# Weight tiles 5 to 7 of the gated unit split beside the spatial products instead of the u products, in the first batch

## Chip, cores and metric

The kernel runs on one core of a Trainium2 chip, as one program launched once. The metric is the device time in microseconds (us) of one execution. Five engines work side by side and each follows its own list of instructions in order: PE (matrix products and their weight loads, PEld), DVE (vector), ACT (scalar, with the table functions), POOL, and SP, which here issues all data transfers (DMA).

## The reference, cut to what matters

Three layers follow each other on 4 batches of 576 positions. The change is in the second; the first runs interleaved with it.

```python
# 1 attention, per batch and head (8 heads of 64), with a causal mask and a decay bias
scores = scale * q @ k.T + min(-(cum_i - cum_j), 0)        # masked above the diagonal
attn = softmax(scores) @ v                                 # -> x, 576 x 512 per batch
# 2 the gated unit
h = gelu(x @ w_in)                                         # w_in 512 x 1024
u, v = h[:, :512], h[:, 512:]
v_n = layernorm(v) * g_ln
v_s = w_sg @ v_n + b_sg                                    # w_sg 576 x 576: the spatial product
x = x + (u * v_s) @ w_out                                  # w_out 512 x 512
# 3 channel mix: k = relu(xk @ w_k), v = (k * k) @ w_v, r = sigmoid(xr @ w_r), out = r * v
```

## The kernel before, in words

Every float32 operand of a product is written as a sum of two parts in a format (fp32r) that PE takes at full pace: a cast gives the high part, a subtraction (`split_lo`, L68 and L69) the low part. A product is then made of three: high by high, high by low, low by high.

The attention of two heads is one pair (`attn_pair`, L205 to L344), 16 pairs in all. The steps of a pair that the prediction names are: the transfer of kq (L217), two splits of it on POOL (L69: qa and KB), two score products per block on PE (L252, L253), the masked minimum on DVE that reads the scores and releases their bank (L277), the exponential on ACT (L285), transposes on PE (L303) with copies back (L305, L307, L313), a reciprocal of the row sums on DVE (L320), its store (L321) and three loads that spread it over the partitions (rb, L324 to L326).

The gated unit is `moe1(b)` (L372 to L480), per batch: v products with layer norm (vn is the normalised v, split in two); four u products, each in two halves of 288 columns (L438 by way of L368), with GELU made of four operations, on ACT and DVE (L499 to L502); then four spatial steps m. Step m makes two product groups sg (L454), evicts each by DVE into a tile ga (L455), multiplies ga by u on POOL (L459), casts it on ACT to gh (L460) and takes the low part gl on POOL (L462). The last loop makes the four output tiles, y, from all gh and gl and the weight tiles 4 to 7 (counted from 0).

The weights of u and of the output stand in eight tiles of 128 columns, index 0 to 3 from w_in and 4 to 7 from w_out. In batch 0 they come as float32 from HBM, are split by the chip and stored to a scratch tensor (`wscr`), from which later batches load them in one transfer (L510). That splitting is `first_wc` (L174 to L191) and `convert` (L74 to L88). It takes tiles 3 to 7 in two halves each. A half is: a transfer `wr` (L188), two activations on ACT that build a rescaled copy `wy` (L76 reads wr, L81 reads wr), two bit operations on DVE (L82 reads wr and wy, L84 works on wy), a cast on ACT into the high half of the tile (L87), and a subtraction on DVE for the low half (L69). After both halves the tile is stored (L190).

Three things set where this work stands. First, tiles ga, wr, wy, y and a few others have one tag, `tmp`, with three buffers: a new tile of the tag takes the buffer of one that has been used up, and its writer waits for the readers of that one. The weight tiles have a tag `wc`, also with three buffers. Second, the program is built by walking `moe1` as a generator, and after each of its steps attention steps of the next batch are added until they have a given share (`attention_until`, L535). Third, a scheduler reorders these instructions on each engine by its own model of their times; the order of the text is only its input. What comes before what on an engine is read from the built program.

In `moe1` before the change, tile m + 3 is made after u product m (L441), for m from 0 to 3, and tile 7 in the loop of output tiles (L465). In later batches the same call is a single load.

Of the kernel before, what the change touches and what calls it, by code (L numbers as in the profile page):

```python
# [37 lines left out]
def fused_kernel(ctx, tc, kqT, vL, s, w_in, g_ln, w_sgT, b_sg, w_out, mu_k, mu_r, w_k, w_v, w_r, out):  # L38
# [25 lines left out]
    def f32(ap):  # L64
        return ap.bitcast(F32)


    def split_lo(eng, lo, x, hi):  # L68
        eng.tensor_tensor(out=lo, in0=x, in1=f32(hi), op=ALU.subtract)  # L69
# [278 lines left out]
    def scale_pending(early):  # L348

        while pending:  # L350
            x_t, rbs = pending.pop()
            i = nc.vector.tensor_tensor(out=x_t, in0=x_t, in1=rbs, op=ALU.mult)
            if early is not None:
                after(i, early)
# [3 lines left out]
    def bank(name, free=True):  # L358

        tag = ('sc', 'tp', 'acc', 'sc', 'tp', 'acc', 'tp', 'acc')[banks[0] % 8] if free else "acc"  # L360
        banks[0] += 1
        return psum1.tile([P, 512], F32, tag=tag, name=name, bufs={'sc': 2, 'tp': 3, 'acc': 3}[tag])
# [9 lines left out]
    def moe1(b):  # L372

        GS = 1.0 if b == B - 1 else 2.0 * WS
        wcs = []
        for c in range(3):
            wcs.append(load_wc(b, c))
        xs = low.tile([P, 2, KD, S], F32R, tag="xs", name=f"xs_{b}")
        xs = [xs[:, i] for i in range(2)]

        xq = ep.tile([P, S + 1], F32R, tag="tmp", name=f"xq_{b}", bufs=3)
        xq = xq[:, :KD * P].rearrange("p (k a t) -> p k a t", k=KD, a=2)
        if pending and pending[0][0] is xT[(b, KD - 1)]:
            scale_pending(None)
        for k in range(KD):
            nc.scalar.copy(xs[0][:, k], xT[(b, k)])
            split_lo(nc.gpsimd, xs[1][:, k], xT[(b, k)], xs[0][:, k])
        for i in range(2):
            nc.vector.tensor_copy(xq[:, :, i], f32(xs[i][:, :, 512:]))
        yield 0  # L390
        v = ep.tile([P, NT, FH], F32, tag="v", name=f"v{b}")
        st6 = ep.tile([P, NT, 6], F32, tag="st6", name=f"st6_{b}")
        mv = ep.tile([P, NT, 2], F32, tag="mv", name=f"mv{b}")
        rstd = ep.tile([P, NT], F32, tag="rstd", name=f"rstd{b}")
        vn = [ep.tile([P, NT, FH], F32R, tag=f"vn{i}", name=f"vn{i}_{b}") for i in range(2)]
        for t in range(NT):
            m = TW[t]
            acc = bank(f"v{b}_{t}", b == B - 1)
            mms = []
            for k in range(KD):  # L400
                if t < 4:
                    xh, xl = (x[:, k, t * P:t * P + m] for x in xs)
                    mms += [(xh, wv[0][:, k]), (xh, wv[1][:, k]), (xl, wv[0][:, k])]
                else:
                    x2 = xq[:, k].rearrange("p a t -> p (a t)")
                    mms += [(x2, wv[0][:, k]), (x2, wv[1][:, k])]
            gemm3(acc, mms)
            if t < 4:
                gelu(b, v[:, t], acc)
            else:  # L410
                xt = ep.tile([P, S + 1], F32, tag="tmp", name=f"vx{b}", bufs=3)
                nc.scalar.copy(xt[:64, :FH], acc[64:128])
                nc.vector.tensor_tensor(out=xt[:64, :FH], in0=acc[:64], in1=xt[:64, :FH], op=ALU.add)
                gelu(b, v[:64, 4], xt[:64, :FH])
            nc.vector.bn_stats(out=st6[:m, t], in_=v[:m, t])
            nc.vector.bn_aggr(out=mv[:m, t], in_=st6[:m, t])
            nc.gpsimd.tensor_scalar_add(rstd[:m, t:t + 1], mv[:m, t, 1:2], LN_EPS * GS * GS)
            nc.gpsimd.tensor_tensor(out=rstd[:m, t:t + 1], in0=rstd[:m, t:t + 1], in1=mhalf[:m, 0:1], op=ALU.pow)
            nc.vector.tensor_scalar(out=v[:m, t], in0=v[:m, t], scalar1=mv[:m, t, 0:1], scalar2=rstd[:m, t:t + 1],
                                    op0=ALU.subtract, op1=ALU.mult)  # L420
            last_cast[0] = nc.scalar.copy(vn[0][:m, t], v[:m, t])
            if t < 4:
                split_lo(nc.vector if b == B - 1 else nc.gpsimd, vn[1][:, t], v[:, t], vn[0][:, t])
            else:

                split_lo(nc.vector, vn[0][64:128, 4], v[:64, 4], vn[0][:64, 4])
            yield len(mms) * 512 * V_W
        u = []
        for m in range(KD):
            u.append(ep.tile([P, S], F32, tag="u", name=f"u{b}_{m}", bufs=4))  # L430
            for hf in range(2):
                acc = bank(f"u{b}_{m}_{hf}", b == B - 1)
                c = slice(hf * HF, (hf + 1) * HF)
                mms = []
                for k in range(KD):
                    wh, wl = wcs[m][:, 0, k * P:(k + 1) * P], wcs[m][:, 1, k * P:(k + 1) * P]
                    mms += [(wh, xs[0][:, k, c]), (wh, xs[1][:, k, c]), (wl, xs[0][:, k, c])]
                gemm3(acc[:, :HF], mms)  # L438
                gelu(b, u[m][:, c], acc[:, :HF])
                yield 12 * 288 * U_W  # L440
            wcs.append(load_wc(b, m + 3))  # L441
        gh = ep.tile([P, KD, S], F32R, tag="v", name=f"gh{b}")
        gs = [[gh[:, m] for m in range(KD)], []]
        for m in range(KD):
            f = slice(m * P, (m + 1) * P)
            ga = ep.tile([P, S + 1], F32, tag="tmp", name=f"ga{b}_{m}", bufs=3)
            for hf in range(2):
                acc = bank(f"sg{b}_{m}_{hf}", b == B - 1)
                c = slice(hf * HF, (hf + 1) * HF)
                mms = []  # L450
                for k in range(4):
                    mms += [(vn[0][:, k, f], wsg[0][:, k, c]), (vn[0][:, k, f], wsg[1][:, k, c]), (vn[1][:, k, f], wsg[0][:, k, c])]
                mms += [(vn[0][:, 4, f], wsg[0][:, 4, c]), (vn[0][:, 4, f], wsg[1][:, 4, c])]
                gemm3(acc[:, :HF], mms)  # L454
                nc.vector.scalar_tensor_tensor(out=ga[:, c], in0=acc[:, :HF], scalar=g_sb[:, m:m + 1], in1=bsg[:, c],  # L455
                                               op0=ALU.mult, op1=ALU.add)
                yield 14 * 288 * S_W
            eng = nc.vector if b == B - 1 else nc.gpsimd
            eng.tensor_tensor(out=ga[:, :S], in0=ga[:, :S], in1=u[m], op=ALU.mult)  # L459
            last_gate[0] = nc.scalar.copy(gs[0][m], ga[:, :S])  # L460
            gs[1].append(ep.tile([P, S], F32R, tag="u", name=f"gl{b}_{m}", bufs=4))
            split_lo(eng, gs[1][m], ga[:, :S], gs[0][m])  # L462
        for m in range(KD):
            if m:
                wcs.append(load_wc(b, m + 6) if m + 6 < 8 else None)  # L465
            y = ep.tile([P, S + 1], F32, tag="tmp", name=f"y{b}_{m}", bufs=3)
            nc.gpsimd.memset(y[:, 0:1], 0.0)
            wc = wcs[4 + m]
            for hf in range(2):
                acc = bank(f"o{b}_{m}_{hf}", b == B - 1)  # L470
                c = slice(hf * HF, (hf + 1) * HF)
                mms = []
                for k in range(KD):
                    wh, wl = wc[:, 0, k * P:(k + 1) * P], wc[:, 1, k * P:(k + 1) * P]
                    mms += [(wh, gs[0][k][:, c]), (wh, gs[1][k][:, c]), (wl, gs[0][k][:, c])]
                gemm3(acc[:, :HF], mms)
                nc.vector.scalar_tensor_tensor(out=y[:, 1 + hf * HF:1 + (hf + 1) * HF], in0=acc[:, :HF], scalar=1.0 / (GS * WS), in1=xT[(b, m)][:, c],
                                               op0=ALU.mult, op1=ALU.add)
                yield 12 * 288 * O_W
            nc.sync.dma_start(out=ydram[m, :, b], in_=y)  # L480
# [23 lines left out]
    def load_wc(b, c):  # L504
        if b == 0:
            if c >= 3:
                first_wc(c)
            return wc0[c]
        wc = ew.tile([P, 2, KD * P], F32R, tag="wc", name=f"wc{b}_{c}", bufs=3)
        nc.sync.dma_start(out=f32(wc.rearrange("p a f -> p (a f)")), in_=f32(wscr[c]))  # L510
        return wc
# [261 lines left out]
    for p in range(TOK // PW):  # L773
# [7 lines left out]
        a, b, c = (psum2.tile([P, 2, 512], F32, tag="ps", name=f"ps{n}_{p}", bufs=4) for n in "abc")  # L781
# [80 lines left out]
```

## Time and profile before

| | |
|---|---|
| device time, median of 3 runs | 683.03 us (681.72 to 685.47) |
| the profiled execution, its device time | 679.44 us |
| its span | 677.7 us |
| PE busy | 645.2 us (95%) |
| DVE busy | 479.1 us (71%) |
| ACT busy | 416.0 us (61%) |
| POOL busy | 219.7 us (32%) |
| mean granted clock of PE, as a share of full speed | 0.988 |

The span runs from the first to the last instruction of the profiled execution, 1.7 us less than its device time. The profiled execution is 3.6 us faster than the median of the runs. Busy shares are means over the span: an engine can be the one that is waited for in one stretch and idle in another, so what this change can do is read from the first batch, some 120 to 190 us into the span.

Three views are used below. A row of the order of time (the timeline) gives an instruction's start in us from the span's start, its duration in us, engine, line, operation, the output and input tiles by the program's names without their numbers, shapes, how many like it in a row (x), and in brackets how long the engine had been idle before and what released it; starts and ends overlap a little, since an engine takes the next instruction while the last one drains. A row of the table of stretches gives, for one stretch, its length and the busy time of PE, PEld, DVE, ACT and POOL with counts, the granted clock of PE, the busy share of the DMA engines and the GB/s. A row of the waits gives who waited for whom, the us in total, how often, and the longest.

### The profile page before, as it was taken

The page shows a single profiled execution, that of the slowest core. Times are in us where ns is not written, and L with a number is a line of the kernel's source. Part 1 is how long each engine was busy: PE and PEld are TensorE (multiplying, and loading weights), DVE is VectorE, ACT ScalarE, POOL GpSimd, SP SyncE. Part 2 cuts the span into 40 slices and gives each one's busy share as a digit, 9 for nine tenths or more (in the row PEclk, how much of TensorE's full clock was granted, in tenths as well). Part 3 has the DMA queues.
Part 4 walks back from the last instruction along what each step waited for, and adds up shares of the span by engine and source line. Part 5 has one row for each costly group of instructions (what it writes and reads, how often), then busy time and mean ns, then how long its engine had stood idle before and what let it go on. Part 6 is the DMA issues. An engine that isn't in the chain of part 4 may idle for free.

```text
span 677.7 us, 11532 instructions
## 1 busy us (share of the span) xinstructions
PE 645.2 (95%) x3912; PEld 553.5 (82%) x3912; DVE 479.1 (71%) x995; ACT 416.0 (61%) x940; POOL 219.7 (32%) x233
## 2 busy tenths in 40 slices
PE   3869999799999999999999999999999999999997
PEld 2547676779878988877988899988888988999997
DVE  7876679986668645469644388787875959677863
ACT  5878777785558656368653285587755779543530
POOL 8556646368436459237363030000000000000000
PEclk9969999999999999999999999999999999999999
DMA  7764652455453532733510675567744593546643
GB/s 227 221 205 140 186 167 73 138 158 158 152 186 102 143 115 55 240 117 90 163 37 15 214 268 183 164 224 222 255 164 163 188 361 136 168 182 195 225 139 117
DMA packets 56459, 112.74 MB, mean 166 GB/s; under 512 B 7680, under 2 KB 20624, under 8 KB 56400
## 3 DMA queue, kind: packets, MB, share of 16 engines
q1 hardware_dynamic: 56400, 112.01, 52.3%
q8 instruction: 31, 0.51, 0.3%
q14 instruction: 28, 0.23, 0.1%
HBM read 74.46 MB, written 28.02 MB: 151 GB/s over the span
## 4 chain that ended last, share of the span: by engine, by line
PE 83%; DVE 6%; DMA 6%; ACT 2%; SPq 1%; issue 1%; POOL 0%; DVEq 0%; ACTq 0%; POOLq 0%
PE k L368 15%; PE sg L368 9%; PE pv L338 8%; PE r L368 7%; PE o L368 7%; PE psa L771 7%; PE u L368 6%; PE v L368 5%; PE tp L303 5%; PE psb L771 4%; PE sc L252 4%; PE sc L253 3%; PE psc L771 2%; DMA kq<-in_kqT_dram 1%; DMA wc<-wscr 1%
## 5 line engine op out<-in xcount | busy, mean ns | idle before, releaser
L368 PE MATMUL k<-x,wk 128*128 128x512 f32 (+1 forms) x480 | 101.4, 372 | 0.0
L368 PEld LDWEIGHTS k<-x,wk 128*128 128x128 f32 x480 | 83.6, 188 | 17.4
L252 PE MATMUL sc<-ka,qa 128*128 128x512 f32 (+3 forms) x180 | 64.0, 366 | 21.6 <-DVE mx L277 10.8
L285 ACT ACTIVATE st<-st,mx 128x128 f32<-128x128 f32 (+4 forms) x124 | 72.0, 582 | 19.3 <-DVE mx L277 18.8
L277 DVE CUSTOM_DVE_ANT_0 st<-sc,mask 128x512 f32<-128x512 f32 (+3 forms) x124 | 61.1, 503 | 27.7 <-PE sc L253 24.4
L368 PE MATMUL sg<-wsg,vn 128*128 128x288 f32 x448 | 65.2, 298 | 0.9 <-DVE u L502 0.9
L338 PE MATMUL pv<-pt,vf 128*64 128x320 f32 (+4 forms) x448 | 64.8, 366 | 0.2 <-ACT pt L305 0.2
L368 PEld LDWEIGHTS sg<-wsg,vn 128*128 128x128 f32 x448 | 60.8, 188 | 1.5 <-DVE u L502 1.1
L252 PEld LDWEIGHTS sc<-ka,qa 128*128 128x128 f32 x180 | 33.9, 189 | 32.1 <-DVE mx L277 15.1
L253 PE MATMUL sc<-KB,QB 128*128 128x512 f32 (+3 forms) x180 | 57.4, 335 | 1.0 <-DVE wv L69 1.0
L338 PEld LDWEIGHTS pv<-pt,vf 128*64 128x64 f32 x448 | 35.5, 137 | 23.5 <-issue 5.2
L303 PE MATMUL tp<-ident,st 128*128 128x128 f32 x300 | 49.5, 282 | 1.2 <-ACT st L285 1.0
L368 PE MATMUL r<-x,wr 128*128 128x512 f32 (+1 forms) x240 | 50.6, 372 | 0.0
L368 PEld LDWEIGHTS r<-x,wr 128*128 128x128 f32 x240 | 41.7, 188 | 8.8
L368 PE MATMUL v<-wv,xs 128*128 128x512 f32 x192 | 48.5, 397 | 0.0
L69 POOL TENSOR_TENSOR qa<-kq,QB 64x576 fp32r<-64x576 f32 x29 | 45.1, 1555 | 3.1 <-POOL st_f L283 1.0
L229 POOL CAST QB<-kq 64x576 fp32r<-64x576 f32 x28 | 21.1, 757 | 73.6 <-PE sc L253 44.3
L69 POOL TENSOR_TENSOR KB<-kq,ka 64x576 fp32r<-64x576 f32 x29 | 43.5, 1499 | 3.9 <-ACT ka L230 1.9
L303 PEld LDWEIGHTS tp<-ident,st 128*128 128x128 f32 x300 | 35.6, 142 | 10.6 <-ACT st L285 4.6
L368 PE MATMUL o<-gh,wc 128*128 128x288 f32 x192 | 40.8, 298 | 0.8 <-DMA wc<-wscr 0.8
L368 PEld LDWEIGHTS v<-wv,xs 128*128 128x128 f32 x192 | 35.1, 188 | 7.5 <-POOL QB L229 0.5
L368 PE MATMUL u<-xs,wc 128*128 128x288 f32 x288 | 40.9, 297 | 0.0
(188 smaller groups left out, 1451.8 us busy)
## 6 DMA issues: line engine op xcount, KB each, us to landing
wc<-wscr SPq DMA_DIRECT2D x24, 512.0 KB
kq<-in_kqT_dram SPq DMA_DIRECT2D x32, 288.0 KB
kr<-kdram SPq DMA_DIRECT2D x12, 768.0 KB
kdram<-k SPq DMA_DIRECT2D x16, 512.0 KB
yt<-ydram SPq DMA_DIRECT2D x24, 257.0 KB
vf<-in_vL_dram SPq DMA_DIRECT2D x16, 320.0 KB
ydram<-y SPq DMA_DIRECT2D x16, 288.5 KB
gt<-gdram SPq DMA_DIRECT2D x12, 384.0 KB
```

What stands on the lines that cost most here:

```text
L69: eng.tensor_tensor(out=lo, in0=x, in1=f32(hi), op=ALU.subtract)
L229: (nc.scalar.copy if hd < 2 else nc.gpsimd.tensor_copy)(qb[64:128], kq[64:128])
L252: nc.tensor.matmul(sc[:m, :c1 - c0], qa[:, q], ka[:, c0:c1], start=True, stop=False)
L253: nc.tensor.matmul(sc[:m, :c1 - c0], qb[:, q], kb[:, c0:c1], start=False, stop=True)
L277: mi = nc.vector.tensor_tensor_reduce(out=st[:, c0:c1], in0=sc[:, :n], in1=mk, op0=ALU.add, op1=ALU.min, scale=-SCALE, scalar=mx[:, 0:1] i ...
L285: e = nc.scalar.activation(st[:, :w], st[:, :w], AF.Exp, bias=mx[:, last:last + 1], scale=-1.0, accum_out=sm[:, i + 5 * (hh == 1):i + 5 * ...
L303: nc.tensor.transpose(tp[:, c:c + P], st[:, j * P:(j + 1) * P], ident)
L338: nc.tensor.matmul(acc[64 * a:64 * a + 64, o:n], vf[:, a, kk], pt, start=(kk == 0), stop=(kk == nk - 1))
L368: nc.tensor.matmul(acc, a, w_, start=(i == 0), stop=(i == n - 1))
L771: nc.tensor.matmul(ps[:, c, :HW], l, r, start=(start and i == 0), stop=(i == len(mms) - 1), skip_group_check=True)
```

## The change

In batch 0, the tiles of index 4, 5 and 6 (the fifth to the seventh) are made after the spatial steps 0, 1 and 2 instead of after the u products 1, 2 and 3. Tile 3 stays behind u product 0, tile 7 stays in the output loop. Batches 1 to 3 are written as before. The line numbers of `gelu`, the evictions and the gate grow by one to three.

```diff
@@ -438,7 +438,8 @@
                 gemm3(acc[:, :HF], mms)
                 gelu(b, u[m][:, c], acc[:, :HF])
                 yield 12 * 288 * U_W
-            wcs.append(load_wc(b, m + 3))
+            if b or m == 0:
+                wcs.append(load_wc(b, m + 3))
         gh = ep.tile([P, KD, S], F32R, tag="v", name=f"gh{b}")
@@ -460,6 +461,8 @@
             last_gate[0] = nc.scalar.copy(gs[0][m], ga[:, :S])
             gs[1].append(ep.tile([P, S], F32R, tag="u", name=f"gl{b}_{m}", bufs=4))
             split_lo(eng, gs[1][m], ga[:, :S], gs[0][m])
+            if b == 0 and m < 3:
+                wcs.append(load_wc(b, m + 4))
         for m in range(KD):
```

The built programs show what this moves. In their rows the name of a tile stands with its own number behind it: wy4_0 is the first half of tile 4, ga0_1 the gate tile of batch 0 and step 1, sc6 the scores of pair 6. The first place is DVE beside the second u product, before the change:

```order
L352 TENSOR_TENSOR xT5_1150<-xT5_1150,rb5_1360 128x576
L82 SCALAR_TENSOR_TENSOR wy4_0_1456<-wr4_0_1455,wy4_0_1456 128x256
L500 SCALAR_TENSOR_TENSOR u0_1_1419<-u0_1_1419,u0_1_1_1437 128x288
L69 TENSOR_TENSOR wcs3_1399<-wy3_1_1410,wcs3_1399 128x256
L84 SCALAR_TENSOR_TENSOR wy4_0_1456<-wy4_0_1456 128x256
L307 COPY pt2_6_1520<-tp6_0_3_1577 128x4x128
L277 ISA st6_2_4_1621,mx6_2_4_1622<-sc6_2_4_1_1629,mask2_123,mx6_2_4_1622 128x64
```

The same place in the changed program:

```order
L352 TENSOR_TENSOR xT5_1150<-xT5_1150,rb5_1360 128x576
L503 SCALAR_TENSOR_TENSOR u0_1_1419<-u0_1_1419,u0_1_1_1437 128x288
L69 TENSOR_TENSOR wcs3_1399<-wy3_1_1410,wcs3_1399 128x256
L69 TENSOR_TENSOR vn0_0_1026<-v0_1022,vn0_0_1026 64x512
L307 COPY pt2_6_1500<-tp6_0_3_1557 128x4x128
L503 SCALAR_TENSOR_TENSOR u0_2_1454<-u0_2_1454,u0_2_0_1455 128x288
L277 ISA st6_2_4_1581,mx6_2_4_1582<-sc6_2_4_1_1589,mask2_123,mx6_2_4_1582 128x64
```

The L82 and the L84 of tile 4 are gone from in front of the score eviction (L277), and the vn split and one more GELU operation stand there.

The second place is ACT at the casts gh, before the change:

```order
L87 CAST wcs6_1702<-wy6_1_1713 128x256
L460 CAST gh0_1722<-ga0_0_1723 128x576
L460 CAST gh0_1722<-ga0_1_1794 128x576
L460 CAST gh0_1722<-ga0_2_1831 128x576
L340 COPY xT7_1862<-pv7_0_2055 128x256
L305 COPY pt1_8_2185<-tp8_0_1_2218 128x384
```

In the changed program the second and the third of them stand here:

```order
L76 ACTIVATE wy5_0_1793<-wr5_0_1792 128x256
L81 ACTIVATE wy5_0_1793<-wr5_0_1792,mhalf_70 128x256
L461 CAST gh0_1662<-ga0_1_1754 128x576
L87 CAST wcs5_1791<-wy5_0_1793 128x256
L230 CAST ka16_2163<-kq16_2158 64x576
L76 ACTIVATE wy5_1_1802<-wr5_1_1801 128x256
L81 ACTIVATE wy5_1_1802<-wr5_1_1801,mhalf_70 128x256
L285 ACTIVATE st7_2_4_1918,sums1_93<-st7_2_4_1918,mx7_2_4_1919 128x576
L87 CAST wcs5_1791<-wy5_1_1802 128x256
L285 ACTIVATE st7_1_0_1985,sums1_93<-st7_1_0_1985,mx7_1_0_1986 128x128
L76 ACTIVATE wy6_0_1950<-wr6_0_1949 128x256
...
L461 CAST gh0_1662<-ga0_2_1811 128x576
```

The cast gh of step 1 stands behind the first half of tile 5, that of step 2 behind the second half and the first of tile 6; before, all weight casts were ahead of the gate casts.

The third place is SP, which issues the transfers, in the changed program; wr4 to wr6 are the halves, rc and rb the reciprocals of attention:

```order
L188 DMA wr4_1_1744<-in_w_out_dram 128x2x256
L217 DMA kq17_2173<-in_kqT_dram 128x576
L321 DMA rdram_65<-rc6_1688 9x128
L324 DMA rb6_1692<-rdram_65 64x576
L325 DMA rb6_1692<-rdram_65 64x512
L326 DMA rb6_1692<-rdram_65 64x64
L188 DMA wr5_0_1792<-in_w_out_dram 128x2x256
L190 DMA wscr_61<-wcs4_1734 128x1024
L239 DMA vf8_2170<-in_vL_dram 128x640
L188 DMA wr5_1_1801<-in_w_out_dram 128x2x256
```

Before, the first half of tile 5 stood ahead of the rc store of pair 6, and that of tile 6 directly behind it; now the first half of tile 5 is behind that store and its three rb loads.

## Rows read from the trace of the kernel before

**Rows 1.** The page's first part: busy time of each engine, share of the span, instructions.

```profile
PE 645.2 (95%) x3912; PEld 553.5 (82%) x3912; DVE 479.1 (71%) x995; ACT 416.0 (61%) x940; POOL 219.7 (32%) x233
```

**Rows 2.** Table of stretches of 10 us, three of them.

```profile
120.00:130.00 10.00, 7.79 (x59) 7.17 (x57) 9.38 (x18) 6.16 (x15) 6.42 (x7) 1.00 0.52 148
130.00:140.00 10.00, 8.80 (x51) 8.15 (x52) 8.65 (x29) 8.78 (x27) 3.01 (x4) 0.83 0.41 124
...
160.00:170.00 10.00, 10.00 (x77) 9.35 (x76) 5.94 (x13) 3.58 (x7) 9.90 (x9) 1.00 0.35 114
```

**Rows 3.** Order of time on PE, from the u products to the output products.

```profile
131.15 0.39 PE L252 MATMUL sc<-ka,qa 128*128 128x256 f32 x1 [3.35 <-DVE mx L277]
...
132.93 3.25 PE L368 MATMUL u<-xs,wcs 128*128 128x288 f32 x12
...
146.36 0.39 PE L252 MATMUL sc<-ka,qa 128*128 128x256 f32 x1 [0.42 <-DVE mx L277]
...
148.16 2.13 PE L368 MATMUL sg<-wsg,vn 128*128 128x288 f32 x14 [0.86 <-DVE u L502]
...
187.84 0.29 PE L368 MATMUL o<-gh,wcs 128*128 128x288 f32 x1
...
188.22 0.48 PE L252 MATMUL sc<-ka,qa 128*128 128x512 f32 x1
```

**Rows 4.** Order of time on DVE, around the waits of PE.

```profile
126.31 0.89 DVE L82 SCALAR_TENSOR_TENSOR wy<-wr,wy 128x256 uint32<-128x256 uint32 x1
...
127.48 1.27 DVE L69 TENSOR_TENSOR wcs<-wy,wcs 128x256 fp32r<-128x256 f32 x1
128.67 1.62 DVE L84 SCALAR_TENSOR_TENSOR wy<-wy 128x256 uint32<-128x256 uint32 x1
...
131.34 0.69 DVE L69 TENSOR_TENSOR vn<-v,vn 64x512 fp32r<-64x512 f32 x1
132.05 0.46 DVE L500 SCALAR_TENSOR_TENSOR u<-u,u 128x288 f32<-128x288 f32 x1
...
146.23 1.51 DVE L82 SCALAR_TENSOR_TENSOR wy<-wr,wy 128x256 uint32<-128x256 uint32 x1
```

**Rows 5.** Order of time on POOL, just before PE goes on at 131.15.

```profile
128.55 1.46 POOL L69 TENSOR_TENSOR qa<-kq,QB 64x576 fp32r<-64x576 f32 x1
```

**Rows 6.** Order of time on ACT: a spatial weight cast, a gate cast, tile 7.

```profile
90.59 0.67 ACT L200 CAST wsg<-wsr 128x576 fp32r<-128x576 f32 x1 [0.70 <-DMA wsr<-in_w_sgT_dram]
...
170.79 0.66 ACT L460 CAST gh<-ga 128x576 fp32r<-128x576 f32 x1
...
179.93 0.44 ACT L76 ACTIVATE wy<-wr 128x256 f32<-128x256 f32 x1 [0.76 <-DMA wr<-in_w_out_dram]
180.28 0.52 ACT L81 ACTIVATE wy<-wr,mhalf 128x256 uint32<-128x256 uint32 x1
```

**Rows 7.** Order of time on DVE: a reciprocal, a fast L82, the last L69.

```profile
144.89 0.94 DVE L320 RECIPROCAL rc<-rc 9x128 f32<-9x128 f32 x1
...
173.91 0.42 DVE L82 SCALAR_TENSOR_TENSOR wy<-wr,wy 128x256 uint32<-128x256 uint32 x1 [2.48 <-POOL gl L69]
...
183.67 0.41 DVE L69 TENSOR_TENSOR wcs<-wy,wcs 128x256 fp32r<-128x256 f32 x1
```

**Rows 8.** Order of time on POOL: the split of gl in step 3.

```profile
171.53 1.42 POOL L69 TENSOR_TENSOR gl<-ga,gh 128x576 fp32r<-128x576 f32 x1 [1.40 <-ACT gh L460]
```

**Rows 9.** Issues of transfers on SP's queue, in order of time.

```profile
87.92 0.33 SPq L196 DMA_DIRECT2D wsr<-in_w_sgT_dram  x1
...
145.86 0.30 SPq L321 DMA_DIRECT2D rdram<-rc  x1
...
148.47 0.58 SPq L326 DMA_DIRECT2D rb<-rdram  x1
...
175.57 0.38 SPq L188 DMA_DIRECT2D wr<-in_w_out_dram  x1
```

**Rows 10.** Waits of PE over the whole span: the last long one.

```profile
PE o L368 <- DMA wc<-wscr: 0.8, 1, 0.8
```

## Prediction

> **What bounds the kernel now.** The page's first part comes first: PE is busy 95% of the span of 677.7 us [rows 1], so the change can win or lose only PE's idle time and the clock. Next, the table of stretches of 10 us shows where idle lies in the first batch: PE is busy 7.79 and 8.80 us of the stretches 120 to 130 and 130 to 140, in the second at a granted clock of 0.83 (a part of it at 1.2 instead of 2.4 GHz); from 160 to 170 it is full and DVE is at 5.94 [rows 2]. The u products are made in the first two, most spatial products in the third. Then the order of time on PE gives the waits: 3.35 us before the score products at 131.15, 0.42 at 146.36, 0.86 at 148.16, all released by DVE; the twelve u products at 132.93 took 3.25 us, the fourteen at 148.16 only 2.13 [rows 3]. DVE's order of time says what stood in front of the release at 131.15: an L82 and an L84 of weight tile 4 (0.89 and 1.62 us) and the last L69 of tile 3 (1.27) [rows 4].
>
> **What the change does.** Tiles 4, 5 and 6 are converted in two halves each; a half is one transfer (SP), L76, L81 and L87 on ACT, and L82, L84 and L69 on DVE. Nothing is added; the order shows these behind evictions of the spatial products instead of between those of u. What each part is worth:
>
> *The wait at 131.15.* On DVE the L82 and the L84 leave (2.51 us) and the L69 of vn and an L500 come ahead of the release (0.69 and 0.46) [rows 4], so it comes about 1.3 us earlier; I take 1.2, PE goes on at 130.0. Bounds: nothing gained, if the vn split then waits for POOL, whose qa split ends at 130.01 [rows 5]; 3.35, if DVE is never late.
>
> *The waits 0.42 and 0.86.* They stand by an L82 of 1.51 us on DVE at 146.23 [rows 4], which goes. Gain 1.28; bounds 0 and 1.28.
>
> *The clock.* 0.17 of 10 us is 1.7 us [rows 2]. A wait of 3.35 came before that fall; behind the one of 0.86 the products at 148.16 ran at full pace [rows 3]. The wait that I leave, 2.15, is between them: I take half the loss as gone, bounds 0 and 1.7.
>
> *The new chain.* This decides how much of that stays. ga, wr and wy tiles share three buffers. In the changed program both halves of wr4 and all ga tiles but the first have one, the first ga and then the four halves of wr5 and wr6 the second, every wy the third. So the halves follow each other: a transfer is issued when L82 of the half before has read its buffer. On ACT the cast gh 1 stands behind L76 and L81 of tile 5, and gh 2 behind those of tile 6; on DVE score evictions stand behind them too. Before, tiles 4 to 6 were loaded beside u and stood in nobody's way here.
>
> A half costs the transfer, 0.44 and 0.52 less their overlap (0.87 from 179.93 to 180.80) on ACT [rows 6], 0.42 for L82 [rows 7] and about 0.3 for three hand-overs (estimate, from the 0.08 between the cast's end at 171.45 and POOL's start at 171.53 [rows 6, 8]). The trace has one awaited transfer of this kind: 4.36 us from the issue at 175.57 to ACT's start at 179.93, just behind a vf load [rows 6, 9]. That is the high end. The low end is 2.67, from the issue of the 288 KB of wsr at 87.92 to ACT's start at 90.59 [rows 6, 9], which moves longer pieces. h, a half, is thus 4.3 to 6.0 us. I take 5.1, a transfer of 3.5: two of the four are issued beside stores of 512 KB or rb loads, as that at 175.57, two are not.
>
> Start of the chain: between 131.15 and the end of the second sg group (148.16 + 2.13) lie 19.1 us, of which 1.3 are waits and 1.7 clock [rows 2, 3]; some 4.0 of the 16.1 of work (scores and transposes of the next pair) come later in the new order, so that group ends at 130.0 + 12.1 = 142.1. Eviction, L84, a score eviction and the reciprocal (0.94 [rows 7]) bring DVE to 144.4. The rc store goes and three rb loads follow; from the store's issue at 145.86 to the end of the last load's at 148.47 + 0.58 were 3.2 us [rows 9]. The first half of wr5 stands behind them on SP: issued at 147.6. The ga tile whose buffer it takes is done by then (1.42 for a POOL operation on such a tile, 0.66 for the cast [rows 6, 8]).
>
> Four halves on, the last L82 of tile 6 is done at 147.6 + 4h. The reciprocal (0.94), L84 and the L87 behind it (0.41 each, taken as long as the L69 of such a half), the gh 3 cast (0.66) and the gl 3 split (1.42) [rows 6, 7, 8] give 3.9 more with the hand-overs: gl 3 at 171.9 for h = 5.1, where it ended at 172.95 before [rows 8]. Tile 7 then waits on SP for a rc store, rb loads and the wscr store behind that reciprocal: 147.6 + 4h + 4.5; two halves and the last L84, L87 and L69 (1.24) bring wcs 7 to 153.3 + 6h, or 183.9, where the last L69 ended at 184.08 before [rows 7]. Half of the last output tile (twelve products, 1.8 us at the pace of the fourteen at 148.16) and two small score products (0.39 for the one at 146.36) come after it [rows 3]: 155.5 + 6h.
>
> *The sum.* Before, the last output product of this batch began at 187.84 [rows 3]; it ends near 188.0, and the new order has about 1.1 us more score work done by then (two wide score products and two narrower ones; the wide one at 188.22 took 0.48 and the next starts inside it [rows 3]), so 189.1 is the point to compare with. 155.5 + 6 x 5.1 = 186.1: 3.0 us earlier. With half the clock loss kept (0.85, it delays the start of the chain), 2.2 us earlier. PE alone, by its three gains, would be 2.5 (clock falls) to 4.2 (it stays) earlier, so the chain takes back about a third. After this PE is full to the end but for 0.8 us [rows 10], so the difference stays. The profiled execution of 679.44 us becomes 677.2. The median of the runs, 683.03, stands 3.6 above it; carried over, 680.8.
>
> **The forecast:** a little less time, not enough to be told from no change: 680.8 us, with 679.7 to 685 as its own bounds. (0.5%, 3.4 us, is about what a measurement of this kernel can tell from no change.)
>
> **Rival 1, slower:** the halves take 6.0 us or more. Then wcs 7 sets PE's time: 155.5 + 36 is 2.4 us late, and a clock that falls as it did at 132.93 adds 1.7: 4.1 us, 687.1. Nothing is left of the gain from h = 5.6 on, and the 0.5% is passed at 5.9 with the clock fallen. For it: the only wr transfer with an awaited end took 4.36 [rows 6, 9], and an L82 can take 1.51 instead of 0.42 [rows 4, 7]. Against: DVE is little over half busy there [rows 2], so a half that has landed is soon taken. The L84 at 128.67, four times as long as others, ends soon after POOL's qa split, which ends at 130.01 [rows 4, 5]; POOL is busy 9.90 of 10 us from 160 to 170 [rows 2]. The Trainium skill, "SBUF — State Buffer", section "SBUF: two separate sides", says that a VectorE operation with two SBUF inputs and a GpSimd operation that reads SBUF exclude each other for a whole instruction; this row agrees. By that rule each L82 would wait some 0.7 us here (half a POOL operation), h would be 5.8 and the sum 685.0.
>
> **Rival 2, faster:** h is 4.9 or less and the clock stays up. PE's own work is then the bound: 1.2 + 1.28 + 1.7 = 4.2 us less, 678.8; if the rest of the wait at 131.15 goes too (2.15), 676.7. For it: the wsr transfer, and the idle of DVE [rows 2, 6, 9]. Against: the chain is serial, and half of its transfers have company on the queue.
>
> That the change does not do what it says is excluded by the order: the L82 of tile 4 stands behind the first spatial eviction.
>
> **How the numbers follow.** Forecast 0.44: h from 5.0 to 5.8, or a shorter one with the clock fallen. Rival 2 0.36: it needs a short h and the clock; the rows hold one transfer of that length [rows 6, 9]. Rival 1 0.20: it needs every half at the length of the longest. Faster by over 0.5% is rival 2, within is the forecast, slower is rival 1. The range, 676.5 to 688, takes in rival 2 to its end and rival 1 at its price; beyond either lies under a tenth.
>
> **What would show it.** PE's wait at 131.15 shorter, near 2 us, and none of 0.86 beside the second sg group; new waits of ACT for a wr transfer (L76) in front of gh 1 and gh 2; PE waits of 1 to 2 us in all between the last sg group and the output products; wcs 7 done near 184. It is wrong if PE has no new wait there and the clock stays at 1.00 (rival 2), or if PE stands over 4 us in this stretch and the clock falls again (rival 1). The chain is wrong if tile 5's first transfer goes out far from 147.6.

## The result, and the profile after

The change made the kernel slower: 686.35 us (median of 17 runs, 683.64 to 687.89) against 681.35 of before, measured beside it (median of 17, 677.35 to 685.47). The ratio is 1.0078, 95% interval 1.0062 to 1.0093, so about 5.0 us. (Ratios leave out runs over 1.5% above the fastest of their kernel; there were two, both in the set of e5 below.) No change in the measurable sense (680.8 us against 683.03) was the forecast.

Where the time went is seen first from two marks on PE: the first v product of batch 0, ahead of the change, and the first k product of the third layer, behind it. Of the kernel before, order of time on PE:

```profile
78.41 1.64 PE L368 MATMUL v<-wv,xs 128*128 128x512 f32 x6
...
431.19 3.43 PE L368 MATMUL k<-x,wk 128*128 128x512 f32 x14
```

Of the changed kernel:

```profile
80.09 1.64 PE L368 MATMUL v<-wv,xs 128*128 128x512 f32 x6
...
437.97 3.43 PE L368 MATMUL k<-x,wk 128*128 128x512 f32 x14
```

The profiled execution of the change started up 1.68 us slower, which is not put down to the change (e3 and e4 below, two kernels that work alike, reach the first mark at 78.64 and 80.22 us), and lost 5.10 us more between the marks: the whole difference of the medians. Times of the trace after are to be read with these 1.68 us in mind.

The tables of stretches, each beginning 41.6 us behind the run's first v product, show that it is a gain and a larger loss. Before, 30 us and the 40 us after them (the first number in a bracket is the count of products that PE ran):

```profile
120.00:150.00 30.00, 25.32 (x171) 22.36 (x169) 27.11 (x69) 23.61 (x66) 17.57 (x16) 0.94 0.49 150
150.00:190.00 40.00, 40.00 (x302) 36.21 (x301) 25.65 (x64) 21.69 (x57) 22.91 (x23) 1.00 0.56 168
```

After:

```profile
121.70:151.70 30.00, 27.67 (x198) 23.96 (x197) 23.38 (x58) 20.16 (x55) 15.86 (x15) 1.00 0.36 107
151.70:191.70 40.00, 36.58 (x249) 31.30 (x249) 29.73 (x67) 24.48 (x64) 25.05 (x23) 0.96 0.58 176
```

In the first stretch PE runs 27 products more, in the second 53 fewer; at 40 us for 302 products (0.13 us each) that is, as an estimate, 3.6 us won and 7.0 us lost. The net, 3.4 of the 5.10 us, is rough, since products differ in width. The clock's fall has moved with it: 0.94 of the first stretch before, 0.96 of the second now.

Two marks more hold the gain and the loss apart: the first spatial product, and the first v product of batch 1 behind the output products. Before:

```profile
139.56 2.01 PE L368 MATMUL sg<-wsg,vn 128*128 128x288 f32 x14
...
188.77 1.52 PE L368 MATMUL v<-wv,xs 128*128 128x512 f32 x6
```

After:

```profile
137.24 2.06 PE L368 MATMUL sg<-wsg,vn 128*128 128x288 f32 x14
...
195.03 2.98 PE L368 MATMUL v<-wv,xs 128*128 128x512 f32 x12
```

Without the 1.68 us, the spatial products begin 4.0 us earlier and batch 1 begins 4.6 us later. So nearly the whole loss arises between these two.

The second view is the share of the chain that ended last, by engine (the page's fourth part). Before, and after:

```profile
PE 83%; DVE 6%; DMA 6%; ACT 2%; SPq 1%; issue 1%; POOL 0%; DVEq 0%; ACTq 0%; POOLq 0%
```

```profile
PE 66%; DVE 14%; DMA 10%; ACT 4%; issue 2%; SPq 2%; POOL 0%; DVEq 0%; ACTq 0%
```

A sixth of the span, some 116 us, has left PE. This does not size the loss: only 31 us of it are the stretch from 152.4 to 183.8 us, where the followed chain of the changed kernel leaves PE (before, it stays on PE from 150 to 190), and most of the rest lies behind the mark of batch 1, where little is lost. What the chain runs through in that stretch, and the rows just ahead of it, stand in the order of time over all engines:

```profile
128.74 1.79 DVE L69 TENSOR_TENSOR vn<-v,vn 64x512 fp32r<-64x512 f32 x1
...
131.87 0.38 PE L252 MATMUL sc<-ka,qa 128*128 128x256 f32 x1 [2.33 <-DVE mx L277]
...
150.40 0.54 SPq L188 DMA_DIRECT2D wr<-in_w_out_dram  x1
...
154.24 0.44 ACT L76 ACTIVATE wy<-wr 128x256 f32<-128x256 f32 x1
...
155.13 1.41 DVE L82 SCALAR_TENSOR_TENSOR wy<-wr,wy 128x256 uint32<-128x256 uint32 x1 [0.96 <-ACT wy L81]
...
156.22 1.63 POOL L69 TENSOR_TENSOR gl<-ga,gh 128x576 fp32r<-128x576 f32 x1
...
156.57 0.38 SPq L188 DMA_DIRECT2D wr<-in_w_out_dram  x1
156.58 1.55 DVE L84 SCALAR_TENSOR_TENSOR wy<-wy 128x256 uint32<-128x256 uint32 x1
...
158.94 0.68 DVE L277 CUSTOM_DVE_ANT_0 st<-sc,mask 128x512 f32<-128x512 f32 x1
...
160.12 2.14 PE L368 MATMUL sg<-wsg,vn 128*128 128x288 f32 x14
...
160.71 1.59 POOL L460 TENSOR_TENSOR ga<-ga,u 128x576 f32<-128x576 f32 x1
...
161.05 0.38 SPq L188 DMA_DIRECT2D wr<-in_w_out_dram  x1
161.06 1.52 DVE L84 SCALAR_TENSOR_TENSOR wy<-wy 128x256 uint32<-128x256 uint32 x1
...
162.18 0.65 PE L338 MATMUL pv<-pt,vf 128*64 128x256 f32 x2
...
164.18 0.43 ACT L76 ACTIVATE wy<-wr 128x256 f32<-128x256 f32 x1 [0.76 <-DVE wcs L69]
...
165.51 0.37 SPq L188 DMA_DIRECT2D wr<-in_w_out_dram  x1
...
166.27 1.43 POOL L69 TENSOR_TENSOR gl<-ga,gh 128x576 fp32r<-128x576 f32 x1 [0.27 <-ACT gh L461]
...
166.86 0.30 PE L252 MATMUL sc<-ka,qa 128*128 128x128 f32 x1 [1.59 <-POOL QB L229]
...
169.96 0.43 ACT L76 ACTIVATE wy<-wr 128x256 f32<-128x256 f32 x1
...
171.92 0.68 DVE L277 CUSTOM_DVE_ANT_0 st<-sc,mask 128x512 f32<-128x512 f32 x1
...
172.50 0.37 ACT L340 COPY xT<-pv 128x256 f32<-128x256 f32 x1 [0.62 <-PE pv L338]
...
172.73 0.92 DVE L456 SCALAR_TENSOR_TENSOR ga<-sg,g_sb,bsg 128x288 f32<-128x288 f32 x2
...
173.28 0.40 PE L368 MATMUL o<-gh,wcs 128*128 128x288 f32 x1 [0.34 <-DVE ga L456]
...
173.58 0.40 DVE L82 SCALAR_TENSOR_TENSOR wy<-wr,wy 128x256 uint32<-128x256 uint32 x1
...
176.65 1.44 POOL L69 TENSOR_TENSOR gl<-ga,gh 128x576 fp32r<-128x576 f32 x1 [1.34 <-ACT gh L461]
...
183.83 0.40 PE L368 MATMUL o<-gh,wcs 128*128 128x288 f32 x1 [0.96 <-DVE y L480]
...
191.94 0.95 DVE L69 TENSOR_TENSOR wcs<-wy,wcs 128x256 fp32r<-128x256 f32 x1
```

Read it in three steps. PE's wait in the u stage is 2.33 us instead of 3.35 [rows 3]. Then the splits of tiles 5 and 6 begin (the L188 at 150.40) and take DVE: an L82 of 1.41 and an L84 of 1.55 us stand ahead of the score eviction (L277) at 158.94. PE's last spatial product ends at 162.3 in this trace. From there on the three banks for such sums are all taken: two hold the products of the last step, whose gate tile is evicted at 172.73 only, and the third an attention product (pv) that was begun at 162.18 and is copied out at 172.50. The first output product comes at 173.28, and until then PE has little but attention's scores and transposes, which wait in their turn for DVE and, at 166.86, for POOL. The buffer that the last gate tile waits for is free from 167.70 (the end of the gl split at 166.27); after that its eviction stands behind score evictions in DVE's list, the last of them at 171.92. Before, spatial products ran until 167.5 and output products from 169.1 on. From 160 to 170 us PE ran 42 products where it had run 77 [rows 2]:

```profile
160.00:170.00 10.00, 7.88 (x42) 5.75 (x41) 8.16 (x23) 7.62 (x25) 7.96 (x7) 0.92 0.59 180
```

It was idle for 2.12 us of these 10 only, so the busy share tells less of the loss than the count does.

### The profile page after: what moved, and what is told of

The parts are those of the page before. It is cut to its first block, busy times and chain, and to the rows that moved or that the text cites. A ratio compares the mean times of both kernels' runs of the same rounds, so it can differ in the third digit from the quotient of the medians.

```text
span 684.5 us, 11538 instructions
## 1 busy us (share of the span) xinstructions
PE 648.2 (95%) x3912; PEld 553.8 (81%) x3912; DVE 484.5 (71%) x995; ACT 416.7 (61%) x940; POOL 219.0 (32%) x233
## 4 chain that ended last, share of the span: by engine, by line
PE 66%; DVE 14%; DMA 10%; ACT 4%; issue 2%; SPq 2%; POOL 0%; DVEq 0%; ACTq 0%
PE k L368 15%; PE r L368 7%; PE psa L774 7%; PE o L368 5%; PE sg L368 5%; PE pv L338 5%; PE v L368 4%; PE psb L774 4%; PE tp L303 4%; PE sc L252 3%; DMA rb<-rdram 3%; PE sc L253 3%; DMA rdram<-rc 2%; PE u L368 2%; PE psc L774 2%
## 5 line engine op out<-in xcount | busy, mean ns | idle before, releaser
L277 DVE CUSTOM_DVE_ANT_0 st<-sc,mask 128x512 f32<-128x512 f32 (+3 forms) x124 | 61.1, 503 | 26.8 <-PE sc L253 23.0
L338 PE MATMUL pv<-pt,vf 128*64 128x320 f32 (+3 forms) x448 | 66.7, 367 | 0.2 <-ACT pt L305 0.2
L69 POOL TENSOR_TENSOR qa<-kq,QB 64x576 fp32r<-64x576 f32 x29 | 44.2, 1526 | 3.6 <-ACT QB L229 1.5
L69 POOL TENSOR_TENSOR KB<-kq,ka 64x576 fp32r<-64x576 f32 x29 | 43.6, 1505 | 4.2 <-ACT ka L230 2.1
```

The lines of the kernel that those rows point to most:

```text
L277: mi = nc.vector.tensor_tensor_reduce(out=st[:, c0:c1], in0=sc[:, :n], in1=mk, op0=ALU.add, op1=ALU.min, scale=-SCALE, scalar=mx[:, 0:1] i ...
L338: nc.tensor.matmul(acc[64 * a:64 * a + 64, o:n], vf[:, a, kk], pt, start=(kk == 0), stop=(kk == nk - 1))
```

## The experiments

Each is timed against the kernel before on the same chip; kernels that ran together share its runs. Ahead of a diff stands which kernel is changed. The runs are called e1 to e15 in the order in which they were made; the third and the fourth run are e3 and e4.

**Is it the shared buffers?** Four runs, e1 to e4, on the tag with three buffers. In the first two the number of buffers goes up:

```diff
-            ga = ep.tile([P, S + 1], F32, tag="tmp", name=f"ga{b}_{m}", bufs=3)
+            ga = ep.tile([P, S + 1], F32, tag="tmp", name=f"ga{b}_{m}", bufs=4)
...
```

(and so at the other six tiles of the tag), in the next two batch 0's ga leaves it:

```diff
+            ga = ep.tile([P, S + 1], F32, tag="tmp" if b else "ga", name=f"ga{b}_{m}", bufs=3 if b else 1)
```

The changed kernel with four (e1):

> The changed kernel with a fourth buffer under the tag tmp, nothing else. Theory 1 (shared buffers): the change wins some 3.7 us in the u stage and loses some 7.4 us from 154 to 190 us of the span, because the gate tiles ga 1 to 3 have to follow each other through one buffer, and the halves of tiles 5 and 6 through another. With a fourth buffer most of the loss goes: 675 to 680 us against 681.4 of before, ratio 0.991 to 0.998; the second eviction of ga 3, at 173.6 in the change, comes before 170, and PE waits under 1.5 us in all between 150 and 190. Theory 2 (places in the lists): the splits stand in front of the gate casts on ACT and of score evictions on DVE, whatever the buffers: 684 to 688, ratio over 1.003. Theory 3 (POOL and DVE): the bit operations on DVE that take 1.4 to 1.6 instead of 0.4 us beside POOL's operations set the chain: 684 to 688 too, with as many long ones as in the change.

Measured: 681.23 us, ratio 1.0002 (0.9988 to 1.0015). The loss against before is gone, and the last gate tile is evicted early, as was expected (from 163.50). But that is not where most of it came back: PE runs 223 products in the first stretch and 256 in the second, against 198 and 249 of the change. The second gain is small; the splits start earlier and the u stage wins more.

The kernel before with four (e2):

> The kernel before with the fourth buffer. It tells what the buffer alone is worth. Theory 1: before, PE has no wait between 150 and 190 us, so the buffer can only act in the u stage: 679 to 683, ratio 0.996 to 1.002; then what the run with the change gains over its own kernel is the buffer's worth for the change alone. If the fourth buffer gives before as much as it gives the change (4 us or more), theory 1 is not shown by the first run.

Measured: 684.15, ratio 1.0046 (1.0028 to 1.0063). A buffer more made before slower, by more than was expected. It is not worth a fixed amount, and the first run alone doesn't show theory 1.

Before, ga alone (e3):

> The kernel before, where the four ga tiles of batch 0 have one buffer of their own, so that the halves of the splits keep three among themselves. Theory 1 in the form that the gate tiles' single buffer is the price: ga 3 is evicted some 4 us later than before (167.5) and the time is 683 to 687, though the splits have more room than ever. In the form that the halves' sharing is the price: 678 to 682. Theories 2 and 3: as before, 680 to 683.

Measured: 680.16, ratio 0.9996 (0.9978 to 1.0013). Here the last gate tile is evicted late too (from 170.16), and the time is that of before. All four gate tiles through one buffer cost nothing: the gates' single buffer by itself is not the price.

The change, ga alone (e4):

> The changed kernel with the same buffer for ga. Its lists of PE, POOL and SP are then those of the third run row by row, and those of DVE and ACT but for two rows that trade places. Theory 1 (the change acts through the shared buffers and in no other way): the same time as the third run, within 0.3%. If the change acts in another way too: over 0.5% slower than the third run.

Measured: 679.75, ratio 0.9973 (0.9958 to 0.9988); the medians of the two runs are 0.06% apart and the intervals overlap. In their two traces POOL and SP have the same rows, one by one, from 30 to 130 us behind the first v product. With ga out of the tag the edit has nothing to act on: it works only by who takes one of the three buffers first. It doesn't place an instruction; it puts ga 0 ahead of wr 4 in the queue for buffers, and the splits' start follows.

**Which of the three tiles, and is it the late gate tile?** The first (e5) gives ga 3 alone a buffer, the others move two tiles (e6) or one (e7):

```diff
+            ga = ep.tile([P, S + 1], F32, tag="ga" if (b, m) == (0, 3) else "tmp", name=f"ga{b}_{m}", bufs=1 if (b, m) == (0, 3) else 3)
```

```diff
-            if b or m == 0:
+            if b or m < 2:
                 wcs.append(load_wc(b, m + 3))
...
-            if b == 0 and m < 3:
-                wcs.append(load_wc(b, m + 4))
+            if b == 0 and m < 2:
+                wcs.append(load_wc(b, m + 5))
```

(tiles 5 and 6; for tile 6 alone the conditions are `m < 3` and, for index 6, `m == 0`.)

> The changed kernel, where only the gate tile of the last spatial step of batch 0, ga 3, has a buffer of its own; every other tile keeps the buffer that it has in the change, all halves of tiles 5 and 6 through one buffer as well. Theory 1a: in the change ga 3 waits for the buffer of ga 2 (gl 2 is split at 167.7 us), so that the two products of step 3, finished by PE at 162.2, stay in two of the three banks until 173.6, and PE has only attention steps left. Then this kernel has the u stage's gain and not the loss: 678 to 682, ratio 0.994 to 1.002 (682.5 at most), ga 3 evicted by 167. Theory 1b: the halves, which follow each other through one buffer, set the end by tile 7: 684.5 to 687, since nothing of that is touched. Theory 2 (the gate casts stand behind L76 on ACT): 684 to 687 too, since gh 1 and gh 2 keep their places.

e5 measured: 684.24, ratio 1.0034 (1.0005 to 1.0063). About half of the loss comes back in the median, but the runs that count lie wide apart (679.01 to 688.5), and the trace is of the fastest of them. In that trace the last gate tile is evicted at 161.12 and the loss between the two marks is gone (352.41 us, before 352.78). Theory 1a can be a part; its size stays open.

> The change for the last two of the three tiles: tile 4 stays beside u, tiles 5 and 6 are made after spatial steps 0 and 1. Three buffers; ga 1 and ga 2 share one, ga 0 and ga 3 have others. Theory 1a: ga 3 doesn't wait for ga 2, so 680 to 683. Theory 2 (each tile moved costs by its places): two thirds of the loss of 5.0, 683.7 to 685.5.

e6 measured: 688.9, ratio 1.0094 (1.0058 to 1.013): no better than the whole change, with two tiles instead of three (the intervals overlap). Order of time over the engines, in an execution of 691.03 us, the slowest of its six:

```profile
161.08 0.33 SPq L190 DMA_DIRECT2D wscr<-wcs  x1
161.47 0.43 SPq L188 DMA_DIRECT2D wr<-in_w_out_dram  x1
...
166.71 0.43 ACT L76 ACTIVATE wy<-wr 128x256 f32<-128x256 f32 x1 [6.78 <-DMA wr<-in_w_out_dram]
...
167.64 0.43 DVE L82 SCALAR_TENSOR_TENSOR wy<-wr,wy 128x256 uint32<-128x256 uint32 x1 [4.48 <-ACT wy L81]
...
169.07 1.34 DVE L69 TENSOR_TENSOR wcs<-wy,wcs 128x256 fp32r<-128x256 f32 x1 [0.47 <-ACT wcs L87]
170.34 0.28 DVE L277 CUSTOM_DVE_ANT_0 st<-sc,mask 128x128 f32<-128x128 f32 x1
...
170.68 0.69 PE L252 MATMUL sc<-ka,qa 128*128 128x384 f32 x1 [5.39 <-DVE mx L277]
```

Here the mechanism lies open. A half's transfer goes out at 161.47 and ACT gets it at 166.71; DVE has stood idle for 4.48 us at that half's L82 and goes through L84 and L69 before it reaches the L277 behind them; PE stands for 5.39 us at the scores that this L277 releases. DVE was free for those 4.48 us, but takes its list in order. In the change itself no wait of this length is seen: between 150 and 173 us DVE stands idle at an L82 for 0.96 us at most (155.13), and PE's longest wait is the 1.59 us at 166.86. So e6 shows how a half can hold PE up; that it did so in the change is seen there only in many short delays.

> The change for one tile: tiles 4 and 5 stay beside u, tile 6 is made after spatial step 0. Three buffers; ga 3 takes the one of ga 0. Theory 1a: 680 to 682.5, as before. Theory 2: a third of the loss, 682.2 to 683.8.

e7 measured: 681.03, ratio 0.9992 (0.9967 to 1.0017): tile 6 alone costs nothing. With e6 the price is that of tile 5's move (and of what follows it), not a third for each tile, so theory 2 as it was put there falls. Nor does the start of the row of halves alone tell it: tile 5's first half is issued 54.8 us behind the first v product before, 61.5 in e6 and 70.3 in the change, and e6 loses no less than the change.

**What makes the row of halves slow?** In e8 the second half's wy gets a buffer of its own; in e9 the gates go to DVE:

```diff
+                own = j == 1 and c in (4, 5, 6)
+                yt = ep.tile([P, S + 1], F32, tag="wy" if own else "tmp", name=f"wy{c}_{j}", bufs=1 if own else 3)
```

```diff
-            eng = nc.vector if b == B - 1 else nc.gpsimd
+            eng = nc.vector if b in (0, B - 1) else nc.gpsimd
```

> The changed kernel, where the second halves wy of tiles 4 to 6 have a buffer of their own; in the change all wy of these tiles go through one, so that L76 of a half waits for the L69 of the half before. The chain of the change from 152 to 184 us runs through L76, L81, L82, L84, L87 and L69 of one half after the other and not through PE. Theory 2b (the splits of tiles 5 and 6 as one chain, that stands in front of score evictions on DVE): with the link cut the chain goes back to PE for most of this stretch, 679 to 683, ratio 0.997 to 1.002. Theory 1a (only the late eviction of ga 3): ga 2 and ga 3 share a buffer here too, so 683.5 to 687.

e8 measured: 685.97, ratio 1.0079 (1.0047 to 1.011). The link by wy, L76 waiting for the L69 of the half before, is not the price.

> The changed kernel with the gate product and the gl split of batch 0 on DVE instead of POOL. Theory 3 (DVE's operations with two inputs stand still while POOL works, 1.4 to 1.6 us instead of 0.4; in the change four of them on the chain between 155 and 164 lose 3.9 us): beside fewer POOL operations fewer are long, and the loss shrinks although DVE gets eight more operations of some 0.7 us: 681 to 684.5. If the long ones don't matter: 686 to 690, since DVE has 6 us more to do in front of its score evictions.

e9 measured: 686.04, ratio 1.0068 (1.0043 to 1.0093). Of the twelve operations L82, L84 and L69 that start between 150 and 176 us, five last over 0.8 us in the change, with 10.20 us for all twelve; here three do, with 7.06. Their length shrank by 3.1 us, eight gate operations came, and the time is about that of the change. Theory 3 is seen in the rows; what it is worth by itself is not shown, since the gate operations came with it.

**Can the u stage's gain be had without the loss?** Tile 4's first operations are placed on ACT behind a tanh of the u stage (`tanhs` collects them in order), once in the fourth run's kernel (e10, index 4), once in the kernel before (e13, index 3):

```diff
+            convert(wc[:, 0, j * w:(j + 1) * w], wc[:, 1, j * w:(j + 1) * w], raw, y, t, nc.vector, low=mhalf[:, 0:1], hold=tanhs[4] if c in (4,) else None)
```

> The fourth run (the change, ga of batch 0 in a buffer of its own) with tile 4's first operations on ACT placed behind the tanh of the third u product's first half, so that the splits leave the u stage as in the change without a shared buffer that delays the gates. Theory 2b: the u stage gains 2 to 4 us as in the change, and the later stages lose no more than in the fourth run: 676 to 679, ratio 0.992 to 0.997. Rival: what the u stage gains is given back, since the same splits then press together before the output stage, as in the run with four buffers: 679.5 to 682.

e10 measured: 685.49, ratio 1.0069 (1.0041 to 1.0096), with 168 and 269 products in the two stretches where the fourth run has 180 and 298. The rival, and worse: by this count not even the first stretch wins. There is no sharing with ga at all, and the loss is there once tile 4 is held back.

> The kernel before, with the first operations of tile 4 on ACT placed behind the tanh of the second u product, so that the L82 and L84 of tile 4 stand right behind the release of the scores that PE waits for at 131 us, and not ahead of it; tiles 5 and 6 stay ahead of the gates' rows. If the gain in the u stage comes from these two operations alone, it is had without the loss: 677 to 680, ratio 0.994 to 0.998. If every delay of tile 4 is given back at the output stage: 681 to 685.

e13 measured: 684.55, ratio 1.0042 (1.0016 to 1.0068), 191 and 267 products against 171 and 302 of before. As in the change, the u stage wins and the next stage loses more.

**The operations on DVE themselves.** In the change (e11), and in the kernel before (e12), tiles 5 and 6 leave out L82, L84 and L69; the low part is a second copy on ACT instead, so these kernels leave out work that the result needs:

```diff
+            if c in (5, 6):
+                nc.scalar.activation(y, raw[:, :, 1].bitcast(F32), AF.Abs, scale=2.0 ** -111)
+                nc.scalar.activation(t, raw[:, :, 0], AF.Identity, bias=mhalf[:, 0:1], scale=2.0 ** -29 * (1 - 2.0 ** -9))
+                for i in range(2):
+                    nc.scalar.copy(wc[:, i, j * w:(j + 1) * w], y)
+                continue
```

> The changed kernel, where the halves of tiles 5 and 6 leave out L82, L84 and L69 on DVE; the low part is a copy on ACT instead (one more operation of 0.41 us there, in place of the subtraction), and transfers, wr, wy and their sharing of buffers stay. Theory 2 (twelve DVE operations of these halves stand in the list between score evictions, each behind its transfer and ACT, and PE has nothing but score products at that time): the loss between 159 and 178 us goes and the u stage's gain of 3.7 stays: 676.5 to 680, ratio 0.992 to 0.998. If transfers, ACT or the buffers make the loss: 683.5 to 687.

e11 measured: 680.45, ratio 0.9988 (0.9964 to 1.0011). Its profile, of an execution 2.2 us below that median, in the same two stretches:

```profile
121.50:151.50 30.00, 29.09 (x210) 25.29 (x208) 22.71 (x59) 20.69 (x56) 15.74 (x16) 1.00 0.39 123
151.50:191.50 40.00, 39.09 (x277) 35.30 (x275) 22.66 (x64) 26.30 (x75) 26.28 (x25) 1.00 0.68 210
```

> The kernel before with the same operations left out, as the base for the run ahead. Theory 2: before, these twelve operations stand beside u and the first spatial products; what they cost there is the second and third wait of PE, 1.28 us together: 679 to 681.5. Then the place after the change costs 4 us or more beyond what the place before costs. If this run gains as much as the one ahead, the twelve operations cost the same at both places and theory 2 falls.

e12 measured: 682.56, ratio 1.0014 (0.9989 to 1.0039): the 1.28 us that were put down to them there did not come. So these twelve operations cost 0.9% in the change (1.0078 to 0.9988, some 6 us) and nothing that can be measured where they stood before. The range that was written for e11 was a little too low, but its two cases lie far enough apart to tell: PE's second stretch goes from 249 to 277 products and the clock stays at 1.00. One thing is not told apart: with them go the times for which they hold wr and wy, so their place in the list and their hold on the buffers are taken away together.

**A third of them off DVE.** The subtraction goes to POOL, for tiles 5 and 6 in the change (e14), for tiles 3 to 6 in the third run's kernel (e15):

```diff
+            convert(wc[:, 0, j * w:(j + 1) * w], wc[:, 1, j * w:(j + 1) * w], raw, y, t, nc.gpsimd if c in (5, 6) else nc.vector, low=mhalf[:, 0:1])
```

> The changed kernel with the subtraction (L69) of tiles 5 and 6 on POOL instead of DVE: four of the twelve DVE operations of e11 leave the list, and nothing is left out. Theory 2: about a third of what e11 got back against the change, 683 to 685, ratio 1.003 to 1.006. If only the sum of all three operations as a chain counts (POOL's subtraction is no shorter): as the change, 685.5 to 688.

e14 measured: 683.67, ratio 1.0039 (1.002 to 1.0059): half of the loss is back, with nothing left out.

> The third run (before, ga of batch 0 in a buffer of its own) with the subtraction of tiles 3 to 6 on POOL. Theory 2: eight operations leave DVE's list in the u and gate stages, at no delay of any tile, so the wait at 131 us gets shorter by the L69 of tile 3 (1.27): 677 to 680.5, ratio 0.994 to 0.999. Rival: POOL's qa and KB splits, which PE waits for, come later behind them: 681 to 684.

e15 measured: 685.43, ratio 1.0055 (1.0036 to 1.0074): slower than even the rival had it. That PE waits for POOL's splits is not seen in the trace: its longest wait in the u stage, 3.65 us, ends with an L502 on DVE. Why the subtraction on POOL costs time here stays open. No version tried beats before by more than the 0.27% of the fourth run, whose twin (the third) shows no gain; neither is held to be better.

## Why the prediction was wrong

- *The wait at 131.15.* Right: PE was to go on at 130.0 and did at 131.87 - 1.68 = 130.19, with 2.15 us of wait forecast and 2.33 measured. The vn split took 1.79 us (128.74) where 0.69 was counted [rows 4].
- *The waits of 0.42 and 0.86.* Right: neither is there. But only the second stood by the L82 at 146.23: that of 0.42 ended at 146.36, when this L82 had just begun, and the reciprocal at 144.89 [rows 7] stood ahead of its release.
- *The clock.* Half the loss was taken as gone. In the u stage all of it went (1.00 in the first stretch), and nearly as much came back later: 0.96 over 40 us is 1.6.
- *PE alone, 2.5 to 4.2 us earlier.* Right: 27 products, some 3.6 us, and 4.0 by the first spatial product.
- *The start of the chain.* 147.6 was said, 150.40 - 1.68 = 148.7 measured.
- *A half, h.* 5.1 us was taken. The first three halves took 6.17, 4.48 and 4.46 us from issue to issue, 5.04 in the mean: right. The fourth took 8.47, from the issue at 165.51 to the end of its L82 at 173.98, and with it the mean is 5.9. The transfer, the disputed term, was not long: the second half's had landed within 2.69 us (156.57 to ACT's L76 at 159.26) and the third's within 3.13, below the 3.5 taken. The fourth half waited in the lists: ACT's L76 stands behind score activations until 169.96 and the L82 behind the gate's eviction until 173.58. The text held that a half that has landed "is soon taken", since DVE is little over half busy there. That was read from a trace in which these operations weren't there; with them DVE is at 29.73 of 40 us instead of 25.65.
- *What the halves hold up.* **This is the step that failed.** The sentence "on DVE score evictions stand behind them too" named the cost and gave it no price. PE was taken to wait for weight tile 7 alone, at the end. It lost its time ahead of that: between 162 and 173 us, at scores and at the last gate tile's eviction, with 42 products from 160 to 170 us where 77 had run. When the fourth half was issued, at 165.51 - 1.68 = 163.8, the row of halves was 0.9 us behind the sum (147.6 + 3 x 5.1 = 162.9), and PE was already short of work. gl 3 was split at 178.09 - 1.68 = 176.4, not 171.9, and tile 7 was done at 192.89 - 1.68 = 191.2, not 183.9; PE never waited for that tile. An h of 5.9 put into the sum would not have mended it: 155.5 + 6 x 5.9 = 190.9 is 1.8 us late, 2.7 with half of the clock loss, about half of the 5.0 measured.
- *From the profile to the median.* The profiled execution was taken to lie 3.6 us below the median, from three runs; of the seventeen the median is 681.35, 1.9 us above it. That shifts 680.8, not the 2.2 us that were to be won.
- *Rival 1* had the sign and nearly the size (4.1 us, measured 5.0), but set its price by four halves of 6.0 us, with transfers of 4.36, and by tile 7. Neither decided, so its nearness is in part luck. Tile 5 and 6's operations on DVE did (e11 against e12).
- *The rule on DVE and POOL.* The trace agrees: the L84 at 156.58 ends at 158.13, 0.28 us behind POOL's split that ends at 157.85, and the one at 161.06 ends at 162.58, 0.28 behind the product that ends at 162.30. The Trainium skill, "SBUF — State Buffer", section "SBUF: two separate sides", gives this as an exclusive lock. The 685.0 that it gave was nearer than the forecast, but by an h of 5.8, and the first three halves took 5.04 with three of their six bit operations long. e9 took 3.1 us of such length away, added gate operations to DVE, and the time stayed: what the rule costs here is not shown.

## What to carry to other kernels

An edit that moves where a tile is made can act through nothing but the order in which tiles take the buffers of a shared tag; look up who gets which buffer ahead of what the edit says. The same operations on an engine that takes its list in order cost nothing measurable where PE had other work (e12), and 0.9% where PE was fed by that engine (e11): price such work by what stands behind it in the list, there, and not by the engine's busy share. A wait that is removed early in a stage is only won if the stage behind it was not using that time: here the versions that won in the u stage by starting the splits later (the change, e8, e9, e13) gave back more at the output stage; with a buffer more (e1) it came out even, and where the splits left DVE (e11) less went back than was won.

## What had not been expected of the hardware

A half's transfer had at most 2.69 us from issue to use in the changed kernel (156.57 to 159.26), and 5.24 in e6 (161.47 to 166.71), where it was issued 0.39 us behind a store of 512 KB; the one awaited transfer that was read from the trace of before had taken 4.36 [rows 6, 9]. No run here separates the store from other traffic of that moment.
